# An attention and FFN kernel: the gate's scales as products of two tables, the weights' scales in two steps, and a new table of the order

## The chip, the cores and the metric

The kernel runs on one core of one Trainium2 chip. The metric is the device time of one execution in microseconds (us). The kernel before took 1134.36, 1135.04 and 1135.3 us in three runs (median 1135.04).

## The reference

```python
# q, k, v: 8 batches, 8 heads, 576 positions, 64 wide, float32
scores = scale * np.matmul(q, k.transpose(0, 1, 3, 2))
thresh = np.max(scores, axis=-1, keepdims=True) - tau
scores = np.where(scores >= thresh, scores, -1000000000.0)
attn = np.exp(scores - np.max(scores, axis=-1, keepdims=True))
attn = attn / (np.sum(attn, axis=-1, keepdims=True) + 1e-09)
x = np.matmul(attn, v)            # heads side by side: 4608 tokens x 512
h = x @ w_in                      # 512 x 2048, float64
g = np.where(h >= 1, h, np.where(h <= -1, 0.0, (h + 1) ** 2 / 4))
return g @ w_out                  # 2048 x 512, float64
```

So each batch has an attention with a softmax over only the scores within tau of the row's largest. Its output is the input of a feed-forward layer (FFN), whose gate is zero, a parabola or the identity.

## The kernel before, in words

All products run in fp16. An operand is scaled by a power of two and split into a high and a low half, and the halves are multiplied in two or three products whose sums make one result. The power of two comes from a sum of squares of the operand. Each batch has such a scale for v, each pair of heads for q and k, and each quarter of w_in and the whole of w_out one for the weights.

Attention works on pairs of heads and parts of the queries (two parts a batch; three in the first batch). A part has several tiles of 128 rows. For a tile, PE makes the scores (qk, L982, into one of two PSUM buffers s), DVE scales them and takes the row's extreme (smax, L999) and the threshold (sthr, L1003), ACT takes the exp (sexp, L1006), DVE masks and sums (smask, L1020) and inverts the sum (sden, L1030), POOL normalizes (snorm, L1038), ACT rounds the high half (shi, L1043), POOL makes the low half (slo, L1046), and SP sends both through a transposing DMA into eT (send, L1068). The buffers in between are rings: e has 4, hl 3, eT 2, sm 6. When a part's tiles have landed, PE multiplies them by V (av, L1146), in two column halves of the array (128*64). A tile of 128 rows that belongs to one head uses the array whole; the tile that holds the rest of both heads uses it in halves. TILE names the tiles that go another way: "T" turns the tile on PE, "S" leaves the masked values in PSUM and makes both halves from there on ACT and DVE.

From the second batch on, q and k are rounded on ACT (L575) into one of two nat buffers, with the low half on POOL (L582), and four DMAs each (L599 for kk, L601 for qq) spread them over the array's halves. V goes through POOL (L648), DVE (L653) and a transposing DMA (L656, vb to vst).

The FFN takes groups of 256 tokens (128 in places). In eight steps over the 2048 hidden features (four for 128 tokens) PE makes h (ffn1, L1218), ACT applies relu and square (L1224, L1227), DVE picks with max and min (gate, L1231), ACT and DVE make the halves (ghi, glo, L1236, L1241), and PE adds the second product up in PSUM (ffn2, L1263). The scales in these steps lie in fcs: four numbers for each batch and each quarter of w_in, used as a column of scalars. f_scale (L938) makes them for one batch: seven small ops, four of which write the four quarters of one of the numbers. FSCALE puts the first batch's on POOL and the others' on DVE.

Weights come in as float64. For each of 16 units of both, bit operations make float32 (letters of SIGN, L753 to L788), PE sums squares (L795), w_scale (L705) makes the scale of a quarter in one op of the plan, and the letters of CONV choose the engines that split the unit: "P", "Q" and "D" begin with a split on POOL (L851), "A" and "G" with a norm on ACT or POOL (L839) and a difference on POOL (L848), "M" with a product on PE (L867).

Every step is an op of a Plan with an engine and an assumed cost. The constants LOAD, WLOAD, QMOVE, KMOVE, SEND and VSEND (L35 to L37) hold what the plan assumes of transfers: the first two numbers are their share of the DMA rings, the third is the time from there to the landing. ORDER (L38) is a table of all op numbers. Plan.order (L319) walks through it with these costs, gives each op a start and each buffer a slot, sorts the ops by start, and the kernel is written out in that order. On the chip every engine runs its own ops in that order, each waiting only for what it needs; an op that waits holds up all behind it on its engine. Where the plan sees PE idle for longer than 0.4 us in the first 200 us, keep_warm (L1294) puts in matmuls of ones.

Of the kernel before, what the change touches and what calls it, by code (L numbers as in the profile page):

```python
# [257 lines left out]
]  # L258
ESC = 2.0 ** 15

TILE = {0: "T", 1: "T"}
# [1091 lines left out]
```

## Time and profile before

| | |
|---|---|
| median of the runs | 1135.04 us |
| the profiled execution | 1136.9 us, its span 1135.1 us |
| mean granted PE clock | 0.997 |
| PE, DVE, ACT, POOL busy | 97%, 80%, 77%, 70% of the span |
| shares of the chain that ended last | PE 61%, DVE 12%, POOL 9%, DMA 7%, ACT 6% |
| transposing sends to eT | 286, median 3.5 us from issue to landing |
| moves to kk and to qq | 112 each, median 2.9 and 2.6 us |
| sends to vst | 28, median 4.6 us |

A row of a timeline gives start, duration, engine, line, operation, what it writes and reads, the shape and a count, and in brackets how long the engine was idle before it and what released it. Rows of groups give a count, the busy time, the mean in ns, and the idle time before. PEclk is the granted TensorE clock as a share of full speed. PEld is the load of weights, which overlaps PE. SPq is SyncE's sequencer, which issues all DMAs. Durations of neighbouring ops overlap a little, so starts are compared.

### The profile page before, as it was taken

What the parts mean: (1) busy time and instruction counts of PE and PEld (TensorE: products, weight loads), DVE (VectorE), ACT (ScalarE), POOL (GpSimd) and SP (SyncE); (2) the same over time, 40 slices, a digit from 0 to 9 for tenths busy, and PEclk for the clock granted to TensorE, in tenths of its full rate; (3) what the DMA queues carried; (4) which work ended last, traced back from release to release, by engine and by line L of the source; (5) the groups of instructions that cost most, each with busy time, mean ns of one, the idle gap of its engine ahead of it and who ended that gap; (6) DMA issues with size and microseconds to landing.
All of it is one profiled execution on the core that took longest, in us unless ns stands there. A gap on an engine that the chain in (4) does not pass through costs nothing.

```text
span 1135.1 us, 27375 instructions
## 1 busy us (share of the span) xinstructions
PE 1098.0 (97%) x9669; PEld 771.3 (68%) x9669; DVE 904.9 (80%) x2701; ACT 869.3 (77%) x1677; POOL 795.6 (70%) x908
## 2 busy tenths in 40 slices
PE   8889999999999999999999999999999999999998
PEld 7556657766776666776777667676667676767674
DVE  5999998987899887898788888887688888887322
ACT  7999768888787887878787779677878876777443
POOL 5999997687666888768767877677678885656000
PEclk9899999999999999999999999999999999999999
DMA  9897999779797989759985999669778996466000
GB/s 335 283 257 128 174 205 182 143 150 198 136 184 136 200 186 200 160 109 174 214 145 95 181 219 180 110 117 168 183 151 167 168 183 120 93 115 114 21 20 20
DMA packets 435931, 179.43 MB, mean 158 GB/s; under 512 B 400464, under 2 KB 407632, under 8 KB 435792
## 3 DMA queue, kind: packets, MB, share of 16 engines
q1 hardware_dynamic: 435792, 177.67, 77.0%
q8 instruction: 76, 1.25, 0.5%
q14 instruction: 63, 0.52, 0.1%
HBM read 45.09 MB, written 9.44 MB: 48 GB/s over the span
## 4 chain that ended last, share of the span: by engine, by line
PE 61%; DVE 12%; POOL 9%; DMA 7%; ACT 6%; issue 4%; SPq 1%; POOLq 0%; DVEq 0%; ACTq 0%
PE acc L1263 24%; PE ph L1218 22%; PE s L982 8%; PE ph L1146 6%; DMA eT<-hl 6%; DVE s L999 3%; POOL hl L1046 3%; DVE e L1020 2%; POOL e L1038 2%; ACT hl L1043 1%; ACT e L1006 1%; DVE ph L1231 1%; PE ph L1297 1%; DVE ga L1241 1%; POOL WI L848 1%
## 5 line engine op out<-in xcount | busy, mean ns | idle before, releaser
L1046 POOL TENSOR_TENSOR hl<-e,hl 128x576 f16<-128x576 f32 x286 | 368.1, 1294 | 118.5 <-ACT hl L1043 106.1
L1218 PE MATMUL ph<-x,WI 128*128 128x256 f16 (+1 forms) x4032 | 400.2, 257 | 3.3 <-DVE x L1158 1.3
L1218 PEld LDWEIGHTS <-WI 128*128 128x128 f16 x4032 | 346.8, 98 | 52.3 <-issue 7.5
L1038 POOL TENSOR_SCALAR e<-e,sm 128x576 f32<-128x576 f32 x286 | 220.4, 775 | 89.5 <-DVE sm L1030 64.5
L1020 DVE SCALAR_TENSOR_TENSOR e<-s,sm,e 128x578 f32<-128x578 f32 x286 | 232.3, 816 | 53.9 <-ACT e L1006 44.9
L999 DVE TENSOR_SCALAR_CACHE_REDUCE s<-s,pc 128x576 f32<-128x576 f32 x288 | 233.6, 818 | 40.9 <-PE s L982 36.4
L1006 ACT ACTIVATE e<-s,sm 128x576 f32<-128x576 f32 x288 | 211.7, 740 | 70.2 <-DVE s L999 50.5
L1043 ACT ACTIVATE hl<-e 128x576 f16<-128x576 f32 x286 | 193.5, 682 | 77.2 <-POOL e L1038 37.9
L1263 PE MATMUL acc<-WO,ga 128*128 128x512 f16 x864 | 205.5, 379 | 0.0
L982 PE MATMUL s<-kk,qq 128*128 128x288 f16 (+3 forms) x1360 | 190.8, 286 | 10.8 <-DVE e L1020 8.4
L982 PEld LDWEIGHTS <-qq 128*128 128x128 f16 (+3 forms) x1360 | 113.6, 99 | 77.1 <-issue 31.5
L1231 DVE SCALAR_TENSOR_TENSOR ph<-ph,fcs,asq 128x512 f32<-128x512 f32 (+1 forms) x160 | 111.6, 699 | 59.9 <-ACT asq L1227 59.2
L1224 ACT ACTIVATE asq<-ph,fcs 128x512 f32<-128x512 f32 (+1 forms) x160 | 115.5, 735 | 35.6 <-PE ph L1218 32.7
L1263 PEld LDWEIGHTS <-ga 128*128 128x128 f16 x864 | 81.9, 98 | 82.9 <-issue 3.7
L1146 PE MATMUL ph<-eT,vst 128*64 128x320 f16 (+2 forms) x1928 | 123.1, 279 | 8.1 <-DMA eT<-hl 4.2
L1146 PEld LDWEIGHTS <-vst 128*64 128x64 f16 x1928 | 99.4, 110 | 30.4 <-issue 18.1
L1227 ACT ACTIVATE asq<-asq 128x512 f32<-128x512 f32 x144 | 90.0, 628 | 2.8
L1241 DVE SCALAR_TENSOR_TENSOR ga<-ph,fcs,ga 128x256 f16<-128x256 f32 (+1 forms) x160 | 70.7, 450 | 23.3 <-ACT WO L1236 9.6
L1236 ACT ACTIVATE ga<-ph,fcs 128x256 f16<-128x256 f32 (+1 forms) x160 | 70.1, 450 | 24.9 <-DVE ph L1231 18.7
L1263 PE MATMUL acc<-WO,gb 128*128 128x512 f16 x306 | 73.2, 379 | 0.0
L582 POOL TENSOR_TENSOR nat<-raw,nat 128x576 f16<-128x576 f32 x52 | 66.9, 1289 | 8.2 <-ACT nat L575 8.1
L1263 PE MATMUL acc<-WO,WI 128*128 128x512 f16 x282 | 67.9, 379 | 0.0
(187 smaller groups left out, 1147.8 us busy)
## 6 DMA issues: line engine op xcount, KB each, us to landing
kk<-nat SPq DMA_DIRECT2D x112, 144.0 KB, 2.9
raw<-in_v_dram SPq DMA_DIRECT2D x32, 288.0 KB, 3.7
raw<-in_q_dram SPq DMA_DIRECT2D x32, 288.0 KB, 3.6
raw<-in_k_dram SPq DMA_DIRECT2D x32, 288.0 KB, 3.6
WO<-in_moe_w_in_dram SPq DMA_DIRECT2D x16, 512.0 KB, 7.8
out_dram<-ob SPq DMA_DIRECT2D x32, 256.0 KB, 2.7
qq<-nat SPq DMA_DIRECT2D x112, 72.0 KB, 2.6
x<-in_moe_w_out_dram SPq DMA_DIRECT2D x10, 512.0 KB, 6.6
```

Of the source, the lines that this page charges most:

```text
L982: T.matmul(ap(s, s_ps)[r, f, :SH], q, k, start=ql == kl == 0, stop=kl == 1)
L999: V.tensor_scalar(sv(), sv(), c[:, 24 + v : 25 + v], None, ALU.mult, ALU.min, accum_out=t[:, 0:1])
L1006: A.activation(ev(), sv(), AF.Exp, bias=ap(m, sm)[:, 0:1], scale=-1.0)
L1020: V.scalar_tensor_tensor(ev(SH + 1), sv(SH + 1), t[:, 2:3], ev(SH + 1), ALU.is_le, ALU.mult, accum_out=t[:, 3:4])
L1038: G.tensor_scalar(ev(), ev(), ap(m, sm)[:, 5:6], ESC, ALU.mult, ALU.mult)
L1043: A.activation(part2(0), ev(), AF.Copy)
L1046: G.tensor_tensor(part2(w), ev(), part2(0), ALU.subtract)
L1146: T.matmul(o[hd * D : (hd + 1) * D, :n], vt[:, k, hd * D : (hd + 1) * D], t[:, kb, hd * n : (hd + 1) * n], start=m == 0, stop=m == len(blo ...
L1218: T.matmul(h[:, i], WTh["i"][:, u, wl * 512 + c * P : wl * 512 + (c + 1) * P], x[:, cc, xl, c0 : c0 + n].rearrange("p (t n) -> p t n", n=P ...
L1224: A.activation(tv()[:, :, c], hv()[:, :, c], AF.Relu, bias=fcs[:, b, q, 2 : 3], scale=fcs[:, b, q, 1 : 2])
L1231: V.scalar_tensor_tensor(hv()[:, :, c], hv()[:, :, c], fcs[:, b, q, 0 : 1], tv()[:, :, c], ALU.max, ALU.min)
L1263: T.matmul(ap(ab, accs), gv(h, gl)[:, x], WTh["o"][:, fc + i, wl * 512 : (wl + 1) * 512], start=fc + i == 0 and m == 0, stop=not left[0] a ...
```

## The change

1. fcs is laid out with its four numbers ahead of the quarters. f_scale makes three one-column ops, then a product of the batch's four numbers with four constants (a new table fk), then one product of a table of the weights (four numbers by four quarters) with these four numbers. Batch scales u and x change places in scs for that.
2. w_scale splits its ops: scales gives the scale and its inverse, a new op halves the rest, with one op over two columns in place of two. What splits the weights waits for scales alone; f_scale and o_scale wait for halves.
3. Letters of CONV and SIGN change, and tile 71 takes the way "S".
4. The third number of every transfer constant grows by 0.3 to 0.55, some others by less, and ORDER is a new table (5442 ops instead of 5441).
5. The warm-up activation writes into junk, and tau lies in a fourth column of tcs.

```diff
-CONV = {"i": "MGGGGPGPPPGPPPPP", "o": "QAPAAPPAPDPDDADD"}
-SIGN = {"i": "NNNDNAANNNNNAAAA", "o": "AAANAAAAADAANAAN"}
+CONV = {"i": "GGMGPGGPPPGPMPPP", "o": "QAPADPPAPDPDDADD"}
+SIGN = {"i": "NNNNAAANNNNNNANA", "o": "AAANAAAAAANAANAAN"}
...
-LOAD, WLOAD = (0.82, 0.75, 1.9), (1.32, 1.28, 2.2)
-QMOVE, KMOVE = (0.33, 0.33, 1.35), (0.64, 0.62, 1.35)
-SEND, VSEND = (1.22, 0.2, 1.8), (1.6, 0.5, 2.0)
+LOAD, WLOAD = (0.84, 0.75, 2.2), (1.36, 1.28, 2.6)
+QMOVE, KMOVE = (0.35, 0.33, 1.7), (0.66, 0.62, 1.7)
+SEND, VSEND = (1.24, 0.2, 2.1), (1.7, 0.5, 2.5)
 ORDER = [
-    58, 0, 60, 56, 54, 856, 861, 851, 59, 866, 61, 4, 57, 5, 2, 872, 55, 42, 1, 62, 63, 858, 857, 64, 80, 859, 863, 862, 864, 75, 43, 853, 81, 83,
...
-TILE = {0: "T", 1: "T"}
+TILE = {0: "T", 1: "T", 71: "S"}
...
-    fcs = cp.tile([P, B, NQ["i"], 4], F32, name="fcs")
+    fcs = cp.tile([P, B, 4, NQ["i"]], F32, name="fcs")
+    fk = cp.tile([P, 2, 4], F32, name="fk")
...
+        for n, x in ((0, -51), (2, 37), (3, 88)):
+            G.memset(fk[:, 0, n : n + 1], 2.0 ** x)
...
             V.tensor_scalar(s[:, 0:1], s[:, 7:8], 2.0 ** -51, None, ALU.mult)
+
+        def halves():
+            V.tensor_scalar(s[:, 4:6].bitcast(U32), s[:, 6:8].bitcast(U32), 1, None, ALU.logical_shift_right)
             V.tensor_scalar(s[:, 1:2], s[:, 6:7], 2.0 ** 51, None, ALU.mult)
-            for x in range(2):
-                V.tensor_scalar(s[:, 4 + x : 5 + x].bitcast(U32), s[:, 6 + x : 7 + x].bitcast(U32), 1, None, ALU.logical_shift_right)
             V.tensor_scalar(s[:, 2:3], s[:, 5:6], 2.0 ** 38, None, ALU.mult)
             V.tensor_scalar(s[:, 3:4], s[:, 4:5], 2.0 ** 89, None, ALU.mult)
...
-        so = plan.op("DVE", 1.06, scales, [ps], uses=[sb])
+        so = plan.op("DVE", 0.56, scales, [ps], uses=[sb])
+        so2 = plan.op("DVE", 0.45, halves, [so])
...
         def f_scale(E, s=s, f=f, wi=wi):
-            u, x, r, rx = (s[:, n : n + 1] for n in (4, 5, 6, 7))
+            x, u, k = s[:, 4:5], s[:, 5:6], fk[:, 0]
             E.tensor_scalar(s[:, 0:1], x, 2.0 ** -80, wi[:, 8, 0:1], ALU.mult, ALU.mult)
-            E.tensor_scalar(f[:, :, 0], wi[:, 0], x, 2.0 ** -51, ALU.mult, ALU.mult)
-            E.tensor_scalar(s[:, 0:1], s[:, 0:1], 1.0, 2.0 ** 66, ALU.min, ALU.mult)
-            E.tensor_scalar(f[:, :, 1], wi[:, 3], r, 2.0 ** 88, ALU.mult, ALU.mult)
-            E.tensor_scalar(f[:, :, 2], wi[:, 2], rx, 2.0 ** 37, ALU.mult, ALU.mult)
-            E.tensor_scalar(f[:, :, 3], wi[:, 1], u, s[:, 0:1], ALU.mult, ALU.mult)
             E.tensor_scalar(s[:, 3:4], u, 2.0 ** 65, wi[:, 8, 1:2], ALU.mult, ALU.mult)
+            E.tensor_scalar(k[:, 1:2], s[:, 0:1], 1.0, 2.0 ** 66, ALU.min, ALU.mult)
+            E.tensor_tensor(fk[:, 1], s[:, 4:8], k, ALU.mult)
+            E.tensor_tensor(f, wi[:, 0:4, :], fk[:, 1, :, None].to_broadcast([P, 4, NQ["i"]]), ALU.mult)
...
-        fscale[b] = plan.join([plan.op(*(("DVE", 2.6, partial(f_scale, V)) if how == "V" else ("POOL", 2.0, partial(f_scale, G))), [h, wends])
+        fscale[b] = plan.join([plan.op(*(("DVE", 1.4, partial(f_scale, V)) if how == "V" else ("POOL", 1.3, partial(f_scale, G))), [h, wends])
...
-                plan.op("SP", 0.55, store, [o], uses=[ob], work=(0.68 * r / P, 0.65 * r / P, 1.05))
+                plan.op("SP", 0.55, store, [o], uses=[ob], work=(0.68 * r / P, 0.65 * r / P, 1.6))
```

Lines of the changed kernel stand two further on from the constants' op on, four further on from w_scale to f_scale, and two further on behind it. The order is shown at three places.

DVE around the third batch's f_scale (the stretch of the trace from 350 us on), before:

```order
L1030 RECIPROCAL sm_126<-sm_126 128x1
L1003 TENSOR_SCALAR sm_125<-sm_125,tcs 128x1
L940 TENSOR_SCALAR scs<-scs,wsc_i 128x1
L941 TENSOR_SCALAR fcs<-wsc_i,scs 128x4
L942 TENSOR_SCALAR scs<-scs 128x1
L943 TENSOR_SCALAR fcs<-wsc_i,scs 128x4
L944 TENSOR_SCALAR fcs<-wsc_i,scs 128x4
L945 TENSOR_SCALAR fcs<-wsc_i,scs 128x4
L946 TENSOR_SCALAR scs<-scs,wsc_i 128x1
L1020 SCALAR_TENSOR_TENSOR e_92,sm_125<-s_61,sm_125,e_92 128x578
```

The same place now:

```order
L1022 SCALAR_TENSOR_TENSOR e_92,sm_122<-s_62,sm_122,e_92 128x578
L1032 RECIPROCAL sm_122<-sm_122 128x1
L1243 SCALAR_TENSOR_TENSOR ga_110<-ph_65,fcs,ga_110 128x2x64 x2
L1243 SCALAR_TENSOR_TENSOR gb_113<-ph_65,fcs,gb_113 128x2x64 x2
L940 TENSOR_SCALAR scs<-scs 128x2
L944 TENSOR_SCALAR scs<-scs,wsc_i 128x1
L945 TENSOR_SCALAR scs<-scs,wsc_i 128x1
L946 TENSOR_SCALAR fk<-scs 128x1
L947 TENSOR_TENSOR fk<-scs,fk 128x4
L948 TENSOR_TENSOR fcs<-wsc_i,fk 128x16
L1001 TENSOR_SCALAR s_62,sm_126<-s_62,pc_117 128x2x288
```

Before, a tile's smask (L1020) stands right behind the seven ops; now the next tile's smax (L1001) stands behind five, and smask ahead of them.

SP around the moves that free the nat buffer of one pair's k (the stretch from 419 to 432 us), before:

```order
L601 DMA qq_82<-nat_76 64x576 x3
L599 DMA kk_78<-nat_77 64x1152 x3
L621 DMA raw_70<-in_v_dram 128x576
L1068 DMA_TRANSPOSE eT_98<-hl_96 128x9x128
L599 DMA kk_78<-nat_77 64x1152
L1288 DMA out_dram<-ob_102 64x512
L1068 DMA_TRANSPOSE eT_98<-hl_97 128x9x128
```

The moves of the same pair now:

```order
L1070 DMA_TRANSPOSE eT_98<-hl_97 128x9x128
L537 DMA raw_75<-in_q_dram 128x576
L601 DMA kk_78<-nat_76 64x1152 x2
L1070 DMA_TRANSPOSE eT_98<-hl_95 128x9x128
L601 DMA kk_78<-nat_76 64x1152 x2
L1070 DMA_TRANSPOSE eT_98<-hl_96 128x9x128
L1290 DMA out_dram<-ob_102 128x512
```

A load and a transpose stood ahead of the fourth move; now one transpose stands between the second and the third.

ACT around the ops that take the nat buffers next, before:

```order
L575 ACTIVATE nat_76<-raw_73 128x576
L1236 ACTIVATE ga_110<-ph_65,fcs 128x256
L1236 ACTIVATE gb_114<-ph_65,fcs 128x256
L575 ACTIVATE nat_77<-raw_74 128x576
L1006 ACTIVATE e_91<-s_61,sm_125 128x2x288
L1043 ACTIVATE hl_96<-e_92 128x576
L1006 ACTIVATE e_94<-s_62,sm_124 128x2x288
```

The same place now (L577 is L575 before, L1008 is L1006, L1226 is the relu):

```order
L577 ACTIVATE nat_77<-raw_70 128x576
L1045 ACTIVATE hl_95<-e_94 128x576
L1008 ACTIVATE e_93<-s_62,sm_125 128x2x288
L1226 ACTIVATE asq_100<-ph_65,fcs 128x512
L1008 ACTIVATE e_91<-s_61,sm_123 128x2x288
L577 ACTIVATE nat_76<-raw_69 128x576
L1229 ACTIVATE asq_100<-asq_100 128x512
```

The buffer that the kk moves free (nat_77 before, nat_76 now) was taken three ops after the other one, ahead of two exps; it is now taken five ops after it, behind two exps.

More of the change, by code (lines that the diff above doesn't have):

```diff
@@ L24 @@
 WIDE = 1
-CONV = {"i": "MGGGGPGPPPGPPPPP", "o": "QAPAAPPAPDPDDADD"}
-SIGN = {"i": "NNNDNAANNNNNAAAA", "o": "AAANAAAAADAANAAN"}
+CONV = {"i": "GGMGPGGPPPGPMPPP", "o": "QAPADPPAPDPDDADD"}
+SIGN = {"i": "NNNNAAANNNNNNANA", "o": "AAANAAAAANAANAAN"}
 QHOW = "DDPDPPDPPPD" + 21 * "P"
@@ L434, in attn_ffn_kernel @@
     sel = cp.tile([P, 3, P], BF16, name="sel")
-    warm = cp.tile([P, 1], F32, name="warm")
-    tau_sb = cp.tile([P, 1], F32, name="tau_sb")
-    tcs = cp.tile([P, 3], F32, name="tcs")
+    tcs = cp.tile([P, 4], F32, name="tcs")
+    tau_sb = tcs[:, 3:4]
     wssq = {w: cp.tile([P, NQ[w]], F32, name=f"ssq_{w}") for w in WT}
@@ L480, in warm_up @@
     def warm_up():
-        A.activation(warm, ones[:, 0:1], AF.Exp)
+        A.activation(junk[:, 0:1], ones[:, 0:1], AF.Exp)
     def tau_consts():
@@ L636, in scales @@
             V.tensor_reduce(s[:, 0:1], stat(sb.slot, NPAIR), AX.X, ALU.add)
-            pow2(s[:, 0:1], s[:, 1:2], s[:, 4:5], s[:, 5:6])
-            V.tensor_scalar(s[:, 2:3], s[:, 5:6], 2.0 ** -51, None, ALU.mult)
+            pow2(s[:, 0:1], s[:, 1:2], s[:, 5:6], s[:, 4:5])
+            V.tensor_scalar(s[:, 2:3], s[:, 4:5], 2.0 ** -51, None, ALU.mult)
         so = VS[b] = plan.op("DVE", 0.82, scales, [ps], uses=[sb])
@@ L722, in w_scale @@
         ps = plan.op("PE", 0.1, sums, [lg, c_op], take=[sb])
-        so = plan.op("DVE", 1.06, scales, [ps], uses=[sb])
+        so = plan.op("DVE", 0.56, scales, [ps], uses=[sb])
+        so2 = plan.op("DVE", 0.45, halves, [so])
         db = plan.buf("dgw")
         dg = plan.op("POOL", 0.35, lambda: G.tensor_scalar(ap(db, dgw), ident, s[:, 0:1], 1.0, ALU.mult, ALU.mult), [so], take=[db])
-        return so, dg, db
+        return so, so2, dg, db
     def add_w(w):
@@ L827, in add_w @@
                 n = u // qn
-                so, dg, db = w_scale(w, n, stats[u : u + qn], gbuf)
-                wscale[w].append(so)
+                so, so2, dg, db = w_scale(w, n, stats[u : u + qn], gbuf)
+                wscale[w].append(so2)
             src, hi, lo = WT[w][:, u + WOFF, :], WTh[w][:, u, :512], WTh[w][:, u, 512:]
@@ L1223, in relu @@
                 for b, c in segs(g):
-                    A.activation(tv()[:, :, c], hv()[:, :, c], AF.Relu, bias=fcs[:, b, q, 2 : 3], scale=fcs[:, b, q, 1 : 2])
+                    A.activation(tv()[:, :, c], hv()[:, :, c], AF.Relu, bias=fcs[:, b, 2, q : q + 1], scale=fcs[:, b, 3, q : q + 1])
             def square(tb=tb):
@@ L1230, in gate @@
                 for b, c in segs(g):
-                    V.scalar_tensor_tensor(hv()[:, :, c], hv()[:, :, c], fcs[:, b, q, 0 : 1], tv()[:, :, c], ALU.max, ALU.min)
+                    V.scalar_tensor_tensor(hv()[:, :, c], hv()[:, :, c], fcs[:, b, 0, q : q + 1], tv()[:, :, c], ALU.max, ALU.min)
             def ghi(hv=hv, gv=gv, g=g, q=q):
@@ L1235, in ghi @@
                     for b, c in segs(g):
-                        A.activation(gv(h, 0)[:, :, c], hv()[:, 2 * h : 2 * h + 2, c], AF.Copy, scale=fcs[:, b, q, 3 : 4])
+                        A.activation(gv(h, 0)[:, :, c], hv()[:, 2 * h : 2 * h + 2, c], AF.Copy, scale=fcs[:, b, 1, q : q + 1])
             def glo(hv=hv, gv=gv, g=g, q=q):
@@ L1240, in glo @@
                     for b, c in segs(g):
-                        V.scalar_tensor_tensor(gv(h, 1)[:, :, c], hv()[:, 2 * h : 2 * h + 2, c], fcs[:, b, q, 3 : 4], gv(h, 0)[:, :, c], ALU.mult, ALU.subtract)
+                        V.scalar_tensor_tensor(gv(h, 1)[:, :, c], hv()[:, 2 * h : 2 * h + 2, c], fcs[:, b, 1, q : q + 1], gv(h, 0)[:, :, c], ALU.mult, ALU.subtract)
             wi = [wlo["i", x] for x in range(q * NCC, (q + 1) * NCC)]
```

437 rows, old and new, of the table ORDER are left out of this document.

## The prediction

> **What bounds the kernel.** I read the page's head first, then the table by stretches, the idle rows of PE, and the chain in front of each.
>
> ```profile
> span 1135.1 us, 27375 instructions
> PE 1098.0 (97%) x9669; PEld 771.3 (68%) x9669; DVE 904.9 (80%) x2701; ACT 869.3 (77%) x1677; POOL 795.6 (70%) x908
> 20.00:40.00 20.00, 15.78 (x143) 12.20 (x142) 18.06 (x56) 18.80 (x40) 18.32 (x31) 0.83 0.98 361
> 40.00:100.00 60.00, 51.65 (x671) 36.47 (x670) 55.73 (x185) 55.10 (x105) 56.06 (x73) 1.00 0.91 225
> 100.00:200.00 100.00, 92.94 (x862) 62.88 (x860) 91.17 (x257) 79.27 (x151) 90.75 (x97) 1.00 0.89 174
> 200.00:720.00 520.00, 510.70 (x4385) 359.97 (x4383) 441.41 (x1328) 417.48 (x810) 389.79 (x423) 1.00 0.86 167
> 720.00:1060.00 340.00, 339.63 (x2883) 238.80 (x2881) 269.46 (x803) 255.31 (x483) 231.93 (x248) 1.00 0.74 138
> 1060.00:1135.00 75.00, 70.33 (x551) 45.56 (x548) 21.11 (x48) 31.36 (x65) 0.00 (x0) 0.99 0.06 19
> ```
>
> The columns are stretch, length, busy time of PE, PEld, DVE, ACT and POOL, then granted clock. There are two regimes. From 40 to 200 us DVE (55.73 of 60, 91.17 of 100) and POOL (56.06 of 60, 90.75 of 100) are about as full as in-order queues get, and PE waits for them. From 200 us PE is the bound: it idles 520 - 510.70 = 9.3 us up to 720, 0.4 us up to 1060, and 4.7 us at the end, where the last rows are stored. So no order can win more than about 9.7 us by removing visible waits after 200 us; beyond that only less PE time helps. The seven longest of those waits:
>
> ```profile
> 218.86 1.72 PE L1146 MATMUL ph<-eT,vst 128*64 128x256 f16 x27 [0.55 <-DMA eT<-hl]
> 355.73 0.65 PE L982 MATMUL s<-kk,qq 128*128 128x288 f16 x4 [0.83 <-DVE e L1020]
> 417.78 1.14 PE L982 MATMUL s<-kk,qq 128*128 128x288 f16 x8 [0.35 <-DMA kk<-nat]
> 432.33 0.65 PE L982 MATMUL s<-kk,qq 128*128 128x288 f16 x4 [1.03 <-DVE e L1020]
> 446.26 1.72 PE L1146 MATMUL ph<-eT,vst 128*64 128x256 f16 x28 [1.06 <-DMA eT<-hl]
> 533.06 1.14 PE L1218 MATMUL ph<-x,WI 128*128 128x256 f16 x9 [0.72 <-DVE pc L556]
> 577.96 1.25 PE L1218 MATMUL ph<-x,WI 128*128 128x256 f16 x10 [1.33 <-DVE x L1158]
> ```
>
> Three name a transfer. Three others (432, 533, 578) name DVE, but the engine that feeds it had stood waiting for a transfer a little earlier:
>
> ```profile
> 430.11 0.68 ACT L575 ACTIVATE nat<-raw 128x576 f16<-128x576 f32 x1 [4.02 <-DMA kk<-nat]
> 523.04 1.23 POOL L648 TENSOR_SCALAR vb<-raw,scs 128x1152 f16<-128x1152 f32 x1 [1.69 <-DMA vst<-vb]
> 574.26 0.68 ACT L1043 ACTIVATE hl<-e 128x576 f16<-128x576 f32 x1 [2.00 <-DMA eT<-hl]
> ```
>
> That makes 0.55 + 0.35 + 1.03 + 1.06 + 0.72 + 1.33 = 5.0 us of PE idle with a late landing behind it. The wait at 355.73 is of another kind, taken up below.
>
> **The change part by part.** The sum is made against the span of 1135.1 us (that execution took 1136.9 in all; the median of the runs shown is 1135.04, so a difference in the span is applied to the median as it stands). Under 0.2%, 2.3 us, a difference can't be told from none.
>
> *Changes of array shape (the new order).* A matmul group of another shape starts late:
>
> ```profile
> 792.40 2.78 PE L1218 MATMUL ph<-x,WI 128*128 128x256 f16 x24
> 795.12 2.09 PE L1146 MATMUL ph<-eT,vst 128*64 128x320 f16 x28
> 1057.21 7.86 PE ph L1218 x72
> ```
>
> 24 FFN matmuls alone take 7.86 / 3 = 2.62 us, but from the group at 792.40 to the attention-times-V group behind it (128*64 instead of 128*128) are 2.72: 0.10 us for the change, which no idle column shows. Counted in the built order of PE, past the point where the trace stands at 200 us, the two-headed score tiles and the V products stand in 49 separate runs before and in 41 after; each run costs a change in and one out, so 98 against 82. 16 x 0.09 to 0.10 = **-1.5 us** on the bound engine. Nothing hides it and nothing can take it back. Before 200 us the count rises from 72 to 77, where PE has idle time; nothing for that.
>
> *The gate's scales of a batch (f_scale).* Seven batches have it on DVE, seven rows each:
>
> ```profile
> L944 DVE TENSOR_SCALAR fcs<-wsc_i,scs 128x4 f32<-128x4 f32 x7 | 5.8, 833 | 0.0
> L943 DVE TENSOR_SCALAR fcs<-wsc_i,scs 128x4 f32<-128x4 f32 x7 | 5.5, 789 | 0.0
> L945 DVE TENSOR_SCALAR fcs<-wsc_i,scs 128x4 f32<-128x4 f32 x7 | 4.7, 664 | 0.0
> L941 DVE TENSOR_SCALAR fcs<-wsc_i,scs 128x4 f32<-128x4 f32 x7 | 3.4, 491 | 0.0
> L940 DVE TENSOR_SCALAR scs<-scs,wsc_i 128x1 f32<-128x1 f32 x7 | 1.4, 200 | 0.0
> L943 DVE TENSOR_SCALAR fcs<-wsc_i,scs x7: 214/670/1277, 110.5 to 929.7; 128x4 f32<-128x4 f32 x7
> L653 DVE SCALAR_TENSOR_TENSOR vb<-raw,scs,vb x28: 799/1068/3233, 119.2 to 986.1; 128x576 f16<-128x576 f32 x28
> ```
>
> One-column ops take 0.20 us. The 128x4 ones take (5.8 + 5.5 + 4.7 + 3.4) / 28 = 0.69 us in the mean, from 0.21 to 1.28 for the same four numbers: they are held up, not slow. With three one-column ops a batch costs about 4 x 0.69 + 3 x 0.20 = 3.4 us. After: three one-column ops and two products of tables, 128x4 and 128x16. No row shows a small product of two SBUF tables; the nearest are the 0.20 of a free op and the 0.69 of a held one, and L653, with two SBUF inputs, stretches from 0.80 to 3.23. So 1.0 to 2.0 us a batch, up to 3.3 if each product meets the worst 128x4 case; I take 2.0, the held op's mean, since POOL is as busy as before. The saving of 1.4 us matters where smask stands behind f_scale and PE waits for it: the 0.83 us at 355.73, right after a block that ran from 350.81 to 354.94:
>
> ```profile
> 350.81 0.20 DVE L940 TENSOR_SCALAR scs<-scs,wsc_i 128x1 f32<-128x1 f32 x1
> 351.60 1.28 DVE L943 TENSOR_SCALAR fcs<-wsc_i,scs 128x4 f32<-128x4 f32 x1
> 352.79 1.32 DVE L944 TENSOR_SCALAR fcs<-wsc_i,scs 128x4 f32<-128x4 f32 x1
> 354.74 0.20 DVE L946 TENSOR_SCALAR scs<-scs,wsc_i 128x1 f32<-128x1 f32 x1
> 114.83 0.89 PE L982 MATMUL s<-kk,qq 64*128 64x288 f16 x6 [1.17 <-DVE e L1020]
> ```
>
> **-0.8 us** (ends 0 and -0.8). The batch at 110 us leaves the wait of the last row; it counts under the early part.
> The page "SBUF — State Buffer" of the Trainium skill, section "Who interferes with whom", says that a DVE op with two SBUF inputs is shut out for the whole of a GpSimd op that reads SBUF; by it the new products stay exposed, and a batch would cost nearer 2.0 than 1.0 us. The spread in L653 agrees with it.
>
> *Order against landings.* The planner's latencies grow by 0.3 to 0.55 us a transfer, and the table was made anew. At the 430.11 wait, SP had a load and a transpose ahead of the last of the four moves that free nat_77, and ACT took that buffer two small ops after nat_76, with two exps right behind the waiting op. Now no load stands among the four moves, and the op that takes the buffer which they free comes four ops later, behind an hl half and both exps: were it to wait as long, smask would have its exps. The planner's numbers and this one place speak for fewer waits; how many other places gain is not to be read off. I take half of the 5.0 us, **-2.5 us**: all of it (-5.0) if the new slack reaches everywhere; 5.0 more if the new table has as many tight places again as it removes and adds. The half is a choice between these ends.
>
> *The early part.* The weights' scales release their users after four small DVE ops instead of nine:
>
> ```profile
> L715 DVE TENSOR_SCALAR wsc_i<-wsc_i 128x1 f32<-128x1 f32 x4 | 0.6, 144 | 0.0
> L774 POOL TENSOR_SCALAR WO<-WO 128x512 uint32<-128x512 uint32 x9 | 5.9, 658 | 4.5 <-DMA WO<-in_moe_w_in_dram 3.9
> L765 POOL TENSOR_SCALAR x<-x 128x512 f32<-128x512 f32 x1 | 0.7, 673 | 0.0
> L848 POOL TENSOR_TENSOR WO<-WO 128x512 f16<-128x512 f32 x5 | 5.8, 1160 | 0.4 <-ACT WO L843 0.4
> L851 POOL TENSOR_SCALAR WO<-WO,wsc_o 128x512 f16<-128x512 f32 x11 | 7.7, 696 | 0.9 <-DVE WO L854 0.6
> ```
>
> 5 x 0.144 = 0.7 us sooner, in five places. New letters in SIGN and CONV: POOL gets three L774 more (+2.0), two L765 less (-1.3), one L848 less (-1.2); one L851 goes and one comes; the first batch's f_scale, on POOL, has five ops instead of seven (-0.5): -1.0 us in all. DVE loses a block of 1.4. Both are the full engines there, with PE behind them: **-1.1 us**, between -3.5 (the 0.7 five times) and +2.6 (a second stretch at half clock, below). One tile's halves move from POOL to DVE and ACT (tile 71); on PE some 10 us of products stand between its scores and the next user of its PSUM buffer, so nothing. One fp32 product less for the weights, 0.2 us of PE before 200 us, nothing.
>
> Sum: -1.5 - 0.8 - 2.5 - 1.1 = **-5.9 us**: span 1129.2, median 1135.04 - 5.9 = **1129.1 us**. The ends: -1.5 - 0.8 - 5.0 - 3.5 = -10.8 (1124.2); -1.5 + 5.0 = +3.5 (1138.5).
>
> **The rivals.**
> *Nothing from the new places (20%).* The table removes old waits behind landings and makes as many; the early engines stay equally full. Left are the shape changes: 1135.0 - 1.5 = 1133.5. For it: the six waits lie behind transfers to eT, kk and vst alike, and a better place is shown for one. Against: that place had the longest wait of them, 4.02 us.
> *Slower: SP and ACT run into more late landings (13%).* ACT's op that takes an hl or nat buffer stands in one queue with the exp and the gate. If it comes to stand closer behind the transposes in the new order, each wait delays smask, and PE with it, as at 432 and 578. Twice the 5.0 us, with f_scale's and the early part's gains lost in the same queues, gives +5.0 - 1.5 = +3.5: 1138.5. It decides once the idle of that kind exceeds 5.0 + 1.5 + 2.3 = 8.8 us. Against: every latency that the planner counts on rose, none fell.
> *The clock (7%).* The order builds 198 warming matmuls instead of 277, 79 of them gone, most between 40 and 65 us.
>
> ```profile
> 28.00:35.20 7.20, 5.47 (x40) 5.05 (x38) 6.26 (x23) 6.08 (x13) 6.45 (x14) 0.53 0.94 325
> ```
>
> Here the clock fell to 0.53 after gaps of over 1 us; 5.47 us of busy PE at half speed is about 2.6 us lost. A second such stretch would cost up to 2.6 us: 1129.1 + 2.6 = 1131.7; it needs four to end slower by 2.3.
> The Trainium skill's page "TensorE: Matmul & The Clock Gate", section "What's actually happening", has the clock halved after one idle window of about 3.4 us; by this rule fewer fillers speak against the change. What speaks against it here is the clock of 1.00 in each later stretch up to 1060 us, with PE busy for 51.65 of 60 us.
>
> **Numbers.** The forecast has 60% (1124 to 1132), the three rivals 40%. Faster by over 0.2% (below 1132.8): 0.60 and part of the clock case, 0.64. Within 0.2%: 0.20. Slower: 0.16, the landings and the worst of the clock. The range, 1124.0 to 1138.5, has these ends.
>
> **What would show it.** Right: the stretch 200 to 720 with PE idle near 6 us instead of 9.3; f_scale's five rows at some 2 us together, no wait of PE behind them; idle behind landings near 2.5 us; PE's busy time after 200 us about 1.5 us less; the mark of 200 us reached about 1 us sooner. Wrong: more idle rows after landings than the six above, clock below 1.00 after 40 us, or products over 1 us each.

## The result and the profile after

The changed kernel takes **1125.34 us** (median of 4 runs, 1123.26 to 1126.63); the kernel before took 1135.17 beside it (4 runs, 1134.36 to 1135.87). The ratio is 0.9912, interval 0.9895 to 0.9929: 8 to 12 us faster, forecast 5.9. The profiled execution took 1125.08 us, with a span of 1123.3, which is 11.8 less than the 1135.1 of before. Two of these 11.8 us belong to the two executions alone: that of before, 1136.9 us, lies 1.7 above its median, that of after 0.3 below its own. Single executions of one kernel lie up to 9 us apart here, so of single spans only the larger differences are read.

The page's head and the stretches of the kernel after (columns as before: stretch, length, busy PE, PEld, DVE, ACT, POOL, granted clock):

```profile
span 1123.3 us, 27200 instructions
PE 1090.7 (97%) x9589; PEld 768.2 (68%) x9589; DVE 898.2 (80%) x2684; ACT 871.8 (78%) x1674; POOL 794.5 (71%) x907
20.00:40.00 20.00, 12.38 (x111) 9.51 (x111) 16.57 (x53) 17.46 (x36) 18.38 (x29) 0.83 0.99 388
40.00:100.00 60.00, 51.07 (x581) 34.79 (x582) 55.62 (x177) 54.46 (x104) 54.77 (x71) 0.94 0.95 218
100.00:200.00 100.00, 95.42 (x906) 65.12 (x906) 93.26 (x271) 82.35 (x155) 93.32 (x99) 1.00 0.91 168
200.00:720.00 520.00, 517.15 (x4471) 366.99 (x4470) 441.87 (x1344) 427.19 (x824) 394.88 (x428) 1.00 0.86 169
```

From 200 to 720 us PE is now idle for 520 - 517.15 = 2.85 us instead of 9.3: 6.45 of the 11.8 us. The other 5.4 are what is left by subtraction: 1.5 for fewer changes of array shape behind 200 us, and 3.9 that are put down to the time before 200 us (e5 below shows 3.2 there). Between 40 and 100 us the clock is 0.94 instead of 1.00: it fell more often, not less.

All rows of PE with a wait of 0.15 us or more from 200 to 720 us, after:

```profile
278.53 2.09 PE L1148 MATMUL ph<-eT,vst 128*64 128x320 f16 x28 [0.71 <-DMA eT<-hl]
352.32 0.68 PE L984 MATMUL s<-kk,qq 128*64 128x288 f16 x8 [0.18 <-DVE e L1022]
417.32 0.21 PE L551 MATMUL ph<-pc,sel 128*128 128x2 bf16 x3 [0.52 <-DVE x L1160]
417.88 2.78 PE L1220 MATMUL ph<-x,WI 128*128 128x256 f16 x24 [0.34 <-DVE pc L558]
527.74 0.65 PE L984 MATMUL s<-kk,qq 128*128 128x288 f16 x4 [0.17 <-DVE e L1022]
640.59 0.21 PE L551 MATMUL ph<-pc,sel 128*128 128x2 bf16 x3 [0.25 <-ACT junk L543]
664.61 2.78 PE L1220 MATMUL ph<-x,WI 128*128 128x256 f16 x24 [0.47 <-DVE WO L1243]
```

They sum to 2.6 us; before, fifteen such rows sum to 9.2. One of the seven names a transfer, and the longest is 0.71 us; before it was 1.33, with three above 1 us. ACT's waits for transfers in the same stretch (total us, times, longest), before and after:

```profile
ACT hl L1043 <- DMA eT<-hl: 20.7, 20, 2.0
ACT nat L575 <- DMA kk<-nat: 4.6, 2, 4.0
```

```profile
ACT hl L1045 <- DMA eT<-hl: 8.7, 13, 1.5
ACT nat L577 <- DMA kk<-nat: 2.0, 2, 1.2
```

ACT waits 10.7 us for these two instead of 25.3. The seven batches' f_scale on DVE (total us, mean ns):

```profile
L948 DVE TENSOR_TENSOR fcs<-wsc_i,fk 128x16 f32<-128x16 f32 x7 | 4.8, 689 | 0.2
L947 DVE TENSOR_TENSOR fk<-scs,fk 128x4 f32<-128x4 f32 x7 | 2.1, 307 | 0.2
L944 DVE TENSOR_SCALAR scs<-scs,wsc_i 128x1 f32<-128x1 f32 x7 | 1.4, 204 | 0.0
L945 DVE TENSOR_SCALAR scs<-scs,wsc_i 128x1 f32<-128x1 f32 x7 | 1.4, 203 | 0.0
L946 DVE TENSOR_SCALAR fk<-scs 128x1 f32<-128x1 f32 x7 | 1.0, 149 | 0.0
```

10.7 / 7 = 1.5 us a batch instead of 3.3.

### The profile page after: what moved, and what is told of

Read it like the earlier page. It is cut to its first block, busy times and chain, and to the rows that moved or that the text cites. A ratio compares the mean times of both kernels' runs of the same rounds, so it can differ in the third digit from the quotient of the medians.

```text
span 1123.3 us, 27200 instructions
## 1 busy us (share of the span) xinstructions
PE 1090.7 (97%) x9589; PEld 768.2 (68%) x9589; DVE 898.2 (80%) x2684; ACT 871.8 (78%) x1674; POOL 794.5 (71%) x907
## 3 DMA queue, kind: packets, MB, share of 16 engines
q8 instruction: 75, 1.23, 0.5%
## 4 chain that ended last, share of the span: by engine, by line
PE 60%; DVE 5%; POOL 4%; DMA 3%; ACT 3%; issue 2%; SPq 1%; ACTq 0%; POOLq 0%; DVEq 0%
PE ph L1220 23%; PE acc L1265 23%; PE s L984 7%; PE ph L1148 6%; DMA eT<-hl 2%; POOL hl L1048 2%; DVE e L1022 1%; DVE s L1001 1%; POOL e L1040 1%; POOL nat L584 1%; ACT hl L1045 1%; SPq L601 1%; DVE ph L1233 1%; SPq L603 0%; ACT asq L1226 0%
## 5 line engine op out<-in xcount | busy, mean ns | idle before, releaser
L1040 POOL TENSOR_SCALAR e<-e,sm 128x576 f32<-128x576 f32 x285 | 218.1, 770 | 84.7 <-DVE sm L1032 61.6
L1001 DVE TENSOR_SCALAR_CACHE_REDUCE s<-s,pc 128x576 f32<-128x576 f32 x288 | 233.7, 819 | 46.5 <-PE s L984 42.1
L1008 ACT ACTIVATE e<-s,sm 128x576 f32<-128x576 f32 x288 | 211.1, 740 | 67.1 <-DVE s L1001 42.4
L1226 ACT ACTIVATE asq<-ph,fcs 128x512 f32<-128x512 f32 (+1 forms) x160 | 115.7, 736 | 35.9 <-PE ph L1220 33.7
L1265 PE MATMUL acc<-WO,WI 128*128 128x512 f16 x294 | 70.8, 379 | 0.0
```

The costliest lines, as they stand in the source:

```text
L1001: V.tensor_scalar(sv(), sv(), c[:, 24 + v : 25 + v], None, ALU.mult, ALU.min, accum_out=t[:, 0:1])
L1008: A.activation(ev(), sv(), AF.Exp, bias=ap(m, sm)[:, 0:1], scale=-1.0)
L1040: G.tensor_scalar(ev(), ev(), ap(m, sm)[:, 5:6], ESC, ALU.mult, ALU.mult)
L1226: A.activation(tv()[:, :, c], hv()[:, :, c], AF.Relu, bias=fcs[:, b, 2, q : q + 1], scale=fcs[:, b, 3, q : q + 1])
L1265: T.matmul(ap(ab, accs), gv(h, gl)[:, x], WTh["o"][:, fc + i, wl * 512 : (wl + 1) * 512], start=fc + i == 0 and m == 0, stop=not left[0] a ...
```

## The experiments

The first theory was that the sequence of the table carries most of the gain; the rival, that the code does (f_scale, the two steps of the weights' scales, the letters in CONV, SIGN and TILE). "Idle" is 520 us minus PE's busy time from 200 to 720 us of the profiled execution, "rest" what is left of the span's difference to before, 1135.1, after the idle's difference to 9.3; it holds the changes of shape too. Both come from one execution of each kernel, and e8's is the slowest of its six (1132.32 us). The last column is the busy time of DVE and POOL from 40 to 100 us.

| kernel | median us (runs) | ratio to before, interval | span | idle | rest | DVE / POOL |
|---|---|---|---|---|---|---|
| before | 1135.17 (4) | | 1135.1 | 9.3 | | 55.7 / 56.1 |
| after | 1125.34 (4) | 0.9912, 0.9895-0.9929 | 1123.3 | 2.9 | -5.4 | 55.6 / 54.8 |
| e1 code of before, new table | 1133.05 (12) | 0.9989, 0.9976-1.0001 | 1129.8 | 4.0 | 0.0 | 52.8 / 53.3 |
| e2 code of after, old table | 1142.48 (6) | 1.0067, 1.0049-1.0084 | 1141.2 | 8.3 | +7.1 | 51.1 / 50.0 |
| e3 before, new f_scale | 1132.51 (12) | 0.9988, 0.9974-1.0001 | 1131.5 | 6.7 | -1.0 | 55.0 / 54.7 |
| e4 after, old f_scale | 1126.90 (6) | 0.9935, 0.9918-0.9952 | 1125.4 | 6.1 | -6.5 | 56.2 / 56.3 |
| e5 after to 200 us, old table behind | 1133.45 (12) | 0.9990, 0.9977-1.0004 | 1130.2 | 6.7 | -2.3 | 56.4 / 56.2 |
| e6 before to 200 us, new table behind | 1131.40 (12) | 0.9973, 0.9959-0.9987 | 1129.7 | 6.9 | -3.0 | 56.2 / 56.2 |
| e7 after, no fillers | 1125.51 (6) | 0.9921, 0.9899-0.9943 | 1124.5 | 3.0 | -4.3 | 54.8 / 53.6 |
| e8 after, more fillers | 1129.08 (6) | 0.9952, 0.9933-0.9970 | 1130.5 | 7.4 | -2.7 | 56.3 / 55.7 |
| e9 after, scales in one step | 1127.29 (6) | 0.9930, 0.9915-0.9946 | 1123.9 | 3.8 | -5.7 | 55.4 / 54.3 |
| e10 after, short first fillers | 1124.67 (6) | 0.9914, 0.9897-0.9931 | 1121.5 | 4.1 | -8.4 | 56.8 / 55.9 |
| e11 after, old letters | 1130.05 (6) | 0.9958, 0.9943-0.9973 | 1129.6 | 4.1 | -0.3 | 51.7 / 50.8 |

The median of before was 1135.10 us beside e1 to e4, 1134.39 beside e5 to e8, 1134.64 beside e9 to e11.

### The code and the table apart (e1, e2)

e1 is the kernel before, with the table and the planner's constants of after:

```diff
-LOAD, WLOAD = (0.82, 0.75, 1.9), (1.32, 1.28, 2.2)
+LOAD, WLOAD = (0.84, 0.75, 2.2), (1.36, 1.28, 2.6)
-    58, 0, 60, 56, 54, 856, 861, 851, 59, 866, 61, 4, 57, 5, 2, 872, 55, 42, 1,
+    56, 0, 60, 54, 58, 861, 851, 856, 57, 4, 61, 866, 55, 5, 2, 877, 59, 887, 1,
...
```

The steps are the same ones with other numbers in the two kernels, so the table is carried over step by step; steps that only one of them has stand right behind the step that they belong to.

> The code of before (its letters, its weights' scales in one step, its seven-op f_scale, tile 71 on POOL) written out in the order of the new table, op by op, with the new transfer constants; one op had to be put off by one place. Theory (the table made most of the 9.8 us: shape changes 16 fewer after 200 us, fewer waits behind landings): 8 us faster than before, about 1127. Rival (the new code made most: f_scale, the early release of the weights' splits, the letters): at most 3 us faster, 1132 or more.

Ratio 0.9989, about 1 us faster and not to be told from none: the rival's figure.

e2 is the kernel after, with the table and the constants of before:

```diff
-LOAD, WLOAD = (0.84, 0.75, 2.2), (1.36, 1.28, 2.6)
+LOAD, WLOAD = (0.82, 0.75, 1.9), (1.32, 1.28, 2.2)
...
```

> The code of after in the order of the old table with the old constants; the five new ops (halves) stand right behind the op that they were split from, and some ten ops of the weights' conversion stand a few places off. Theory (the table made most): 1.5 to 2.5 us faster than before, about 1133, with 98 changes of shape after 200 us and ACT waiting about 20 us for landings from 200 to 720 us as before. Rival (the code made most): 6 us or more faster, 1129 or less.

Slower by 0.67% than the kernel before. Neither theory gave that: table and code are worth 1 us and -7.6 us alone and 10 together. The table by itself does cut PE's idle from 200 to 720 us (4.0 us in e1). What e2 loses lies before 200 us: a group of score products that starts at 217.54 in the kernel before starts at 222.70 in e2, 5.2 us later, of 6.1 at the end. What e1 has less than the kernel after lies on both sides: the V product at 278.53 in the kernel after starts 3.3 us later in e1, and the span is 6.5 longer. The stretch from 40 to 100 us, first of e1, then of e2:

```profile
40.00:100.00 60.00, 49.31 (x578) 34.18 (x577) 52.80 (x172) 54.27 (x103) 53.25 (x71) 0.91 0.83 209
```

```profile
40.00:100.00 60.00, 52.04 (x563) 34.26 (x562) 51.09 (x164) 49.87 (x93) 50.00 (x65) 0.86 0.85 211
```

DVE and POOL, which were full there in both parents, stand empty for 3 to 6 us more. These are in-order queues whose steps now seem to meet others that are not ready; which ones is not traced here. PE's 52.04 us in e2 hold fillers and a lower clock (0.86). Behind 200 us e2 has one wait that neither parent has, and e5 has it too (below). So a second theory: **an order is worth its gain only for the engines' letters that it was made with.** A rival for part of the loss is the number of filler matmuls, since keep_warm fills the gaps that the plan sees: 240 in e1 and 309 in e2, against 277 before and 198 after. It is taken up with e11.

### f_scale (e3, e4)

e3 puts the new f_scale into the kernel before, with the layout of fcs, the constants and the fifth point of the change; e4 puts the old one into the kernel after, with the new layout. The lines of e3, which e4 has the other way round:

```diff
-            E.tensor_scalar(f[:, :, 0], wi[:, 0], x, 2.0 ** -51, ALU.mult, ALU.mult)
-            E.tensor_scalar(f[:, :, 1], wi[:, 3], r, 2.0 ** 88, ALU.mult, ALU.mult)
...
+            E.tensor_tensor(fk[:, 1], s[:, 4:8], k, ALU.mult)
+            E.tensor_tensor(f, wi[:, 0:4, :], fk[:, 1, :, None].to_broadcast([P, 4, NQ["i"]]), ALU.mult)
```

> The kernel before with only f_scale's products of tables (and the layout of fcs that they need); order, letters and fillers as before. Theory (f_scale is worth one late wait of 0.8 us and something of the early one): 0.5 to 1.5 us faster, 1134. Rival (DVE's relief of 1.4 us a batch reaches PE in most batches): 3 us or more faster.

> The kernel after with only the seven-op f_scale put back, in the place of the five ops of the new order. Theory (the new order has slack behind it, f_scale worth about 1 us): 0 to 1.5 us slower than after, 1125.5 to 1127. Rival (it is worth 3 us or more): 1128.5 or more, with a wait of PE of about 1 us behind several of its blocks.

e3's ratio is 0.9988 (about 1.4 us faster, 0 to 3): the theory's figure, though not to be told from none. e4's is 0.9935 against 0.9912, 2.6 us slower with overlapping intervals; that is between the two theories, while its median, 1126.90, is 1.6 us slower and in the theory's range. So f_scale is worth 1 to 3 us by the best figures of both, and neither is well clear of nothing. In e4 one long wait of PE stands behind the old block. DVE's rows of e4:

```profile
344.39 1.15 DVE L945 TENSOR_SCALAR fcs<-wsc_i,scs 128x4 f32<-128x4 f32 x1
346.16 1.34 DVE L948 TENSOR_SCALAR fcs<-wsc_i,scs 128x4 f32<-128x4 f32 x1
348.13 0.20 DVE L950 TENSOR_SCALAR scs<-scs,wsc_i 128x1 f32<-128x1 f32 x1
349.73 0.42 DVE L1162 SCALAR_TENSOR_TENSOR x<-ph,x 128x256 f16<-128x256 f32 x1
```

and PE's, which waits for the last of them:

```profile
350.19 1.72 PE L1150 MATMUL ph<-eT,vst 128*64 128x256 f16 x28 [0.86 <-DVE x L1162]
```

In the kernel after the same product starts at 350.42 without a wait. So in e4's profile f_scale's price is paid in one place of the stretch; the rest of e4's idle (6.1 against 2.9) is in waits elsewhere that no row ties to f_scale.

### The two halves of the table (e5, e6)

e5 is the kernel after, with the steps that stand ahead of 200 us as in its table and all others in the sequence of before; e6 is the kernel before, with its own first steps and all others in the sequence of after. Each table begins as its parent's:

```diff
 ORDER = [
     56, 0, 60, 54, 58, 861, 851, 856, 57, 4, 61, 866, 55, 5, 2, 876, 59, 886, 1, 62, 63, 881, 64,
...
```

> The code of after; its order up to the point that the trace reaches at about 200 us, and from there the old table's order, 98 changes of shape there again. Theory (after 200 us the new order is worth some 5 us: 1.5 in shape changes, the rest in waits behind landings; the rest of the 9.8 us is f_scale and an early part that fits its own letters): 5 to 6 us slower than after, 1130.5 to 1131.5, PE idle from 200 to 720 us back at 7 us or more. Rival (the loss of the first two exchanges was of code and order that don't fit anywhere, so the late order alone is worth little): under 2.5 us slower, 1128 or less.

> The code of before, its order up to about 200 us, and the new table's order from there, 82 changes of shape. Theory: 4 to 6 us faster than before, 1129 to 1131, though the old f_scale stands in an order that was made for a shorter one. Rival: under 2.5 us faster, 1132.6 or more.

The new second half alone gains 0.27% (3.1 us, 1.5 to 4.7): a real gain, but short of the 4 to 6 us expected, and between them and the rival's 2.5. The new first half alone gains 0.1%, not to be told from none, against 4 us expected: a miss of theory and rival alike. Its gain is there at first: the score products that start at 217.54 in the kernel before start at 214.30 in e5, 3.2 us sooner, and from there on the two have nearly the same sequence on PE. Alone the halves are worth 1.1 + 3.1 = 4.2 of the 10 us. Part of the difference can be pointed at: each mixture has waits of PE that neither parent has. DVE and PE in e5:

```profile
268.55 0.65 PE L960 MATMUL s<-kk,qq 128*128 128x288 f16 x4
271.73 0.65 PE L960 MATMUL s<-kk,qq 128*128 128x288 f16 x4 [2.52 <-DVE hl L1043]
```

```profile
270.87 0.81 DVE L1043 SCALAR_TENSOR_TENSOR hl<-s,sm,hl 128x576 f16<-128x576 f32 x1
```

and PE in e6:

```profile
237.59 0.21 PE L525 MATMUL ph<-pc,sel 128*128 128x2 bf16 x3 [1.57 <-DVE WI L1217]
251.61 2.09 PE L1122 MATMUL ph<-eT,vst 128*64 128x320 f16 x28 [2.03 <-DVE WI L1217]
```

The first is tile 71, whose low half DVE makes from PSUM since the change: it holds its score buffer 2.5 us longer than the old sequence allows for. In the kernel after DVE runs the same op, and the next scores on PE start without a wait:

```profile
271.71 0.82 DVE L1067 SCALAR_TENSOR_TENSOR hl<-s,sm,hl 128x576 f16<-128x576 f32 x1 [0.50 <-ACT hl L1064]
```

```profile
272.71 0.65 PE L984 MATMUL s<-kk,qq 128*128 128x288 f16 x4
```

The two mixtures' own waits are 2.5 + 1.6 + 2.0 = 6.1 us, which with the 4.2 makes 10.3: enough for the 10, but worked out from two single profiles, not shown.

### The letters and the two steps (e11, e9)

e11 is the kernel after with the letters of before for the weights, and its table carried over to their numbers of the steps:

```diff
-CONV = {"i": "GGMGPGGPPPGPMPPP", "o": "QAPADPPAPDPDDADD"}
+CONV = {"i": "MGGGGPGPPPGPPPPP", "o": "QAPAAPPAPDPDDADD"}
-SIGN = {"i": "NNNNAAANNNNNNANA", "o": "AAANAAAAANAANAAN"}
+SIGN = {"i": "NNNDNAANNNNNAAAA", "o": "AAANAAAAADAANAAN"}
```

> The kernel after with its order, and the letters of the kernel before for the engines of the weights' conversions and signs (a few conversions of the stage before 200 us then go to another engine than the one that the order was made with). Theory (an order is worth its gain only with the letters that it was made for): 3 to 7 us slower than the kernel after, 1128 to 1132, all of it in TensorE's idle time before 200 us, and the idle time behind 200 us within 1.5 us of the kernel after's. Rival (the letters carry nothing, the sequence does): within 1.5 us of the kernel after.

5.2 us slower than the kernel after (0.9958 against 0.9912), though only 11 of the 64 letters differ, and the idle from 200 to 720 us is 4.1 against 2.9. The second theory's figures hold; the rival falls. The loss lies before 200 us, as expected: the V product at 278.53 in the kernel after starts at 284.34 in e11, 5.8 us later, and the span is 6.3 longer.

Fillers are at most a small part of it. e11 has 226 of them. Those that end just as a real operation starts, and so may have held it up, take 12.3 us in e11 and 10.4 in the kernel after, a difference of 1.9 us (in e2 13.9, against 13.2 before). 0.8 of the 1.9 are the first block, the same 95 matmuls, which took 8.05 us instead of 7.21.

PE, DVE, POOL and ACT in e11, a fence each, show one place where the letters act:

```profile
46.35 1.12 PE L837 MATMUL ph<-WI,dgw 128*128 128x512 f32 x2 [1.43 <-DVE WI L764]
50.81 0.16 PE L687 MATMUL ph<-ssq_i,ones 128*128 128x1 bf16 x1 [3.12 <-DVE ssq_i L684]
```

```profile
45.61 0.69 DVE L764 SCALAR_TENSOR_TENSOR WI<-WO,ph 128x512 uint32<-128x512 uint32 x1 [0.90 <-ACT ph L756]
47.90 0.69 DVE L764 SCALAR_TENSOR_TENSOR WI<-WO,ph 128x512 uint32<-128x512 uint32 x1 [0.81 <-ACT WO L747]
```

```profile
46.27 1.28 POOL L560 TENSOR_TENSOR qq<-raw,qq 128x576 f16<-128x576 f32 x1 [2.42 <-ACT qq L553]
```

```profile
44.96 0.62 ACT L756 ACTIVATE ph<-WO 128x512 uint32<-128x512 uint32 x1
45.51 0.67 ACT L553 ACTIVATE qq<-raw 128x576 f16<-128x576 f32 x1
46.66 0.62 ACT L756 ACTIVATE ph<-WO 128x512 uint32<-128x512 uint32 x1
```

The letters of SIGN put the op on a unit's low words (L756) on ACT at other units than the sequence was made for. ACT has four of them from 42 to 47 us; the kernel after has two from 39 to 42 and the next at 46.70. The rounding of q, L553 here, starts at 45.51 instead of 41.71, POOL waits 2.42 us for it, DVE 0.90 and 0.81 us for ACT's work on the weights, and PE 3.12 us for DVE. Here ops of 0.6 us that stand at another place of one queue make waits of 0.8 to 3.1 us in the next ones. The whole loss is not shown by this place: PE is 3.2 us behind the kernel after ahead of it (38.79 instead of 35.60, where a tile is turned), 2.8 at the wait of 3.12 us (50.81 instead of 47.98, since the kernel after waits in this stretch too), and 5.8 only later. So the letters are shown to carry the loss, and its path only in part.

e9 is the kernel after with all instructions of the weights' scales in the first step:

```diff
             pow2(stat(sb.slot, 1), s[:, 5:6], s[:, 6:7], s[:, 7:8])
             V.tensor_scalar(s[:, 0:1], s[:, 7:8], 2.0 ** -51, None, ALU.mult)
-        def halves():
             V.tensor_scalar(s[:, 4:6].bitcast(U32), s[:, 6:8].bitcast(U32), 1, None, ALU.logical_shift_right)
...
+        def halves():
+            pass
```

> The kernel after, with the second step of the weights' scales put back into the first: one step issues all the instructions again, and the other is empty. Theory (the early gain comes from an order that fits the code as a whole, and the first products do wait for the scales now and then): 0.5 to 2.5 us slower than the kernel after's 1125.3, that is 1126 to 1128, with 0.5 to 2 us more of TensorE's idle time before 100 us. Rival (the scales lie beside other work): within 0.5 us of the kernel after, and the idle time before 100 us the same.

0.9930 against 0.9912: 2 us slower in the medians, as the theory has it, but the intervals overlap, and its profile shows none of the 0.5 to 2 us of idle time before 100 us that the theory asked for (PE idle 20.1 us against 19.9 in the kernel after; that execution, 1125.69 us, is one of the two fastest of e9's six). What the two steps are worth stays open, between nothing and 3 us or so.

### The fillers and the clock (e7, e8, e10)

Three kernels are the kernel after with one line changed each: e7, e8 and e10, in this order.

```diff
-        left = gaps(order)
+        left = []
...
-WARM = (0.4, 200, 0.75, 0.056)
+WARM = (0.2, 200, 1.3, 0.056)
...
-                    found += [(free, bank, min(gap, end - free)) for q, y, bank in banks if (q, y) == (p, x)]
+                    found += [(free, bank, min(gap, end - free) - (1.8 if not found else 0)) for q, y, bank in banks if (q, y) == (p, x)]
```

> The kernel after without its 198 matmuls of ones, all else the same. Theory (PE waits for the other engines up to 200 us, so a lower clock there is partly hidden): the clock falls to half for 20 us or more before 100 us, and the kernel is 1 to 4 us slower than after. Rival (the clock is hidden altogether before 100 us): within 1 us of after.

> The kernel after with more matmuls of ones (gaps of 0.2 us up, filled to the full instead of three quarters: 284 in all). If the two shorter stretches at half clock of after (3.4 us each, from 43 and 88 us) cost something, 1 to 2 us faster than after with one stretch left; the rival: the clock is hidden or fillers hold PE up as much, within 1 us of after or slower.

> The kernel after, with the first block of its filler matmuls 1.8 us shorter, so that TensorE's first transpose may start up to 2 us sooner than 9.4 us. Theory (the stretch before 60 us ends with the conversions and loads that other engines do, not with TensorE): first operation near 7.5 us, and the time within 1 us of the kernel after's 1125.3. Rival (the fillers hold the first operation, and what it starts is late by as much for good): 1.2 to 2 us faster, 1123.3 to 1124.1, the best of all kernels.

Without any filler (e7) the time can't be told from the kernel after's, 0.9921 against 0.9912 with overlapping intervals, though the clock is far lower:

```profile
20.00:40.00 20.00, 14.12 (x79) 9.64 (x79) 17.34 (x53) 17.91 (x36) 18.30 (x30) 0.57 1.00 390
40.00:100.00 60.00, 50.73 (x548) 33.08 (x547) 54.80 (x176) 53.16 (x101) 53.57 (x69) 0.89 0.90 221
```

Taking the fillers away also lets PE start sooner, so two effects are in that sum, and the traces show both: against the kernel after, PE in e7 is 2.0 us ahead at its first real operation (7.43 instead of 9.38), 2.6 behind at the V product at 80.76 (78.16), and 0.8 ahead at the V product at 277.73 (278.53). So whatever the low clock cost up to 80 us was made good by 278; that this is because PE waits for other engines there is likely, not shown.

With 86 more fillers than the kernel after (e8) it is 4.5 us slower (0.9952; 3.7 by the medians), not faster. The first rows of PE in e8:

```profile
2.33 8.99 PE L1299 MATMUL ph<-ones 128*128 128x128 bf16 x127 [2.33 <-POOL ones L467]
11.16 0.17 PE L632 MATMUL ph<-vssq,ones 128*128 128x4 bf16 x1
```

The longer first block puts PE's first real operation at 11.16 us, 1.8 later than in the kernel after. But that is not shown to be e8's loss: e10, where it stands at 8.02, gains nothing that can be told (0.9914, 1124.67 us, the lowest median of all, with nearly the interval of the kernel after). In e8's profile PE is 2.1 us behind the kernel after at the row that stands at 417.32 there (419.46), and 7.2 at the end; the 5 us between are lost where neither kernel has a filler, in an execution that was the slowest of six. Where e8 loses stays open.

## Why the prediction was right, and where its sizes were not

The direction and the main path, fewer waits of PE behind 200 us, were right. The time fell inside the range, but 3.8 us from the sum of 5.9: every term but the first came out too small, f_scale's by the least, and 1125.3 us is near the low end, 1124.2, which adds up the best ends of all terms. That so wide a range held is in part luck.

**The bound.** Right: from 200 us PE's waits were what could go, and 6.45 of 9.3 us went. The ceiling, 9.7 us of idle behind 200 us plus shape changes, held too; the rest came from before 200 us.

One reading of it was wrong. The seven waits shown as the longest are not: this row of before is longer than four of them, and one of 0.55 us at 678.31 is left out too.

```profile
397.53 2.09 PE L1146 MATMUL ph<-eT,vst 128*64 128x320 f16 x28 [1.00 <-DVE s L999]
```

Eight rows, 3.4 us in all, stand in no term of the sum. In the kernel after, the rows that name no transfer sum to 1.9 us, so some 1.5 us that the prediction did not count may have gone there.

**Changes of array shape, -1.5.** Right, and the traces have it. Behind 200 us they show 104 changes before and 88 after, where the prediction counts 98 and 82: 16 fewer either way. A change makes the next matmul later by 0.09 to 0.10 us in each pair of medians (kernel after, behind 200 us, PE never idle in between): from the last matmul of a group to the next group it takes 0.216 us without and 0.309 with a change behind the FFN's second product, 0.122 and 0.216 behind scores, 0.106 and 0.205 behind a V product of 256 columns. The sign that I named, 1.5 us less busy time of PE, does not show in the sums: with the fillers taken off, PE is busy for 1076.6 us before (1098.0 - 21.4) and 1076.4 after (1090.7 - 14.3), and in that lie the longer operations at the lower clock as well.

**f_scale, -0.8.** Mechanism right, size probably low. I took 2.0 us a batch; it is 1.5. In the code of before (e3) the two products take longer:

```profile
L946 DVE TENSOR_TENSOR fcs<-wsc_i,fk 128x16 f32<-128x16 f32 x7 | 6.9, 988 | 0.2
L945 DVE TENSOR_TENSOR fk<-scs,fk 128x4 f32<-128x4 f32 x7 | 4.4, 634 | 0.2
```

There a batch is 0.99 + 0.63 + 0.20 + 0.20 + 0.15 = 2.2 us. The duration depends on what POOL does beside them. In the kernel after:

```profile
347.24 1.28 POOL L1048 TENSOR_TENSOR hl<-e,hl 128x576 f16<-128x576 f32 x1
347.32 1.23 DVE L948 TENSOR_TENSOR fcs<-wsc_i,fk 128x16 f32<-128x16 f32 x1
285.17 0.17 DVE L948 TENSOR_TENSOR fcs<-wsc_i,fk 128x16 f32<-128x16 f32 x1
```

The product of 1.23 us starts while a POOL op runs and ends with it; four of the seven L948 do so, and the other three, with no POOL op running as they start, take 0.17 us. The Trainium skill, "SBUF — State Buffer", section "Who interferes with whom", has a DVE op with two SBUF inputs contend with a GpSimd op that reads SBUF. This trace agrees with it.

The bound of 0 to -0.8 counted only the one PE wait behind a block; the best figures of e3 and e4 are 1.4 and 1.6 to 2.6 us. In e3 nothing of it lies before 200 us: the score products at 217.54 in the kernel before start at 217.56.

**Order against landings, -2.5.** Right in kind, too small. Of the 5.0 us of idle behind late landings, 0.7 are left by name (278.53), so up to 4.3 went; ACT's waits for hl and nat fell by 14.6 us. The half that I chose was the weak step. e6, with the new sequence behind 200 us alone, gains 3.1 us, of which 1.5 are the shape changes.

**The early part, -1.1.** The step that failed. It is 3.9 us by subtraction and 3.2 by e5's row. The -1.1 stands beside 1.0 us for POOL and 1.4 for DVE without a working, and I priced the letters by the busy time that they move between the two. e11 shows that with this order they are worth 5, by what waits for what; e1 and e2, that the order alone gains nothing that can be told, and the code alone loses. The second end, 2.6 us for another stretch at half clock, is not borne out by e7. Two small readings were off as well: the product that the weights lose is one of 0.38 us in fp16, and tile 71 costs PE nothing in the new order but 2.5 us in the old one (e5).

**The rivals.** Nothing from the new places: ACT's waits refute it. Late landings: refuted by the same rows. The clock: what it foresaw came (0.94 from 40 to 100 us, where I had named a clock below 1.00 as a sign of being wrong), and its price did not: e7 has a far lower clock and no loss that can be told. The Trainium skill's page "TensorE: Matmul & The Clock Gate", section "What's actually happening", has an idle window halve the clock; the rows of e7 (0.57 and 0.89 without fillers) agree. That fewer fillers must therefore cost time does not follow here: in e7 PE had made up for it by 278 us.

## What to carry to other kernels

A table of the order and the choice of engines are one thing: tried one by one, both can look worthless or harmful (1 us and -7.6 us here) and be worth 10 together, so judge them as a pair, and make the order anew after any change of an engine's letter. Where full in-order queues feed each other, price a moved operation by who waits behind it and not by its own duration. To find where a mixture loses, compare the start of the same PE group in both traces: it told the loss before 200 us from the one behind. A stall behind a late landing on an engine that looks idle enough (ACT, busy for 80% from 200 to 720 us) was worth looking for: the busy shares hid it, the waits by cause showed it.
